# Linear attention followed by a gated feed-forward: even column blocks, cast loads, one-source preps and q prepared a block early

## The chip, the cores and the metric

The kernel runs on one core of a Trainium2 chip. The metric is device time in microseconds (us) from start to end of one execution; lower is better. TensorE (PE in the profile) multiplies, VectorE (DVE), ScalarE (ACT) and GpSimd (POOL) work element by element, SyncE (SP) issues DMAs. PE reads its operands from SBUF and writes to PSUM; DVE and ACT empty PSUM.

## The reference, cut to what matters

```python
# q, k, v: [8 batches, 8 heads, 576 rows, 64]; all float32
def phi(x, c, s):                    # c = cos, s = sin of the row's position
    r = np.maximum(x, 0.0)
    return np.concatenate([r * c, r * s], axis=-1)
q_p, k_p = phi(q, cos_w, sin_w), phi(k, cos_w, sin_w)
kv  = np.einsum('bhsf,bhsd->bhfd', k_p, v)
num = np.einsum('bhsf,bhfd->bhsd', q_p, kv)
den = np.einsum('bhsf,bhf->bhs', q_p, np.sum(k_p, axis=2))[..., None] + 1e-06
x = (num / den) ...                  # -> [4608 tokens, 512]
g = x @ w_gate                       # 512 -> 1536
out = (gelu(g) * (x @ w_val)) @ w_out    # 1536 -> 512
```

The 8 batches of 576 rows give 4608 tokens, and the feed-forward works on 9 blocks of 512 of them. Batch and block borders do not coincide, which is what half of the change is about.

## The kernel before

Words used below: a **prep** is relu times cos or sin (q or k to `qp`, `kp`). **Turning** q means transposing `qp` to `qT`, by a transposing DMA or on PE. **kv** is the k-v product, a **numerator** (`nm`) one of the five 128-row tiles of a batch, which DVE divides into `x_sb`, PE transposes and ACT copies to `xT`. A **gate unit** (`gv`) is one 128-wide slice of the hidden layer: 8 matmuls, gelu on ACT, product on DVE into `hT`. An **output step** is a third of an output tile: 4 matmuls.

```python
def cast_w(i):                                   # weights come as fp32 and are cast
    nc.scalar.copy(wg_sb[:, :, sl], wstage["wgf", i][:, :, 0:n * 128])
    nc.gpsimd.tensor_copy(wv_sb[:, :, sl], wstage["wvf", i][:, :, 0:n * 128])

def prep(name, b, pair, part, n=1):              # two sources in SBUF: src and the table
    for m in range(pair, pair + n):
        nc.vector.scalar_tensor_tensor(
            dst[:, m, :, part * D:(part + 1) * D], src[:, m % 2]..., 0.0,
            tab[:, :, None].to_broadcast([128, R, D]), op0=ALU.max, op1=ALU.mult)

def turn_q(b, pair0, n):                         # two transposing DMAs on SP
    for i in range(2):
        nc.sync.dma_start_transpose(out=qT[b][i]..., in_=src[64 * i:64 * i + 64, ...])

def gv_unit(c0, n, jt):
    gv_ps = psf.tile([128, 2, BLK], FP32, name="gv_ps")   # two buffers
    ...                                          # 4 gate and 4 value matmuls
    nc.scalar.activation(gel[:, 0:n], g_ps[:, 0:n], AF.Gelu)
    ...
    nc.vector.tensor_mul(hT[hb][:, jt, c:c + m], gel[:, o:o + m], v_ps[:, o:o + m])

# ... batch 0: preps, kv, all five tiles, then:
for jt in range(JT):                             # 12 gate units of columns 0 to 575
    gv_unit(0, 288, jt)
    gv_unit(288, 288, jt)
    ...                                          # casts; from jt 8 on: preps of batch 1, turn_q(1)
kv_unit(1)
attend_burst(1)                                  # batch 1 with nothing beside it
for i in range(4):
    o_part(i, range(JT), True)
segs = [(576, 448)] + [(BLK * i, BLK) for i in range(2, 9)]
for si, (c0, n) in enumerate(segs, start=1):
    b = si + 1                                   # the batch attended inside this block
    for jt in range(JT):
        gv_unit(c0, n, jt)
        s = jt - off                             # off: 3 in the first of them, else 0
        if s == 0: prep_pairs("qp", b, 0)
        if s == 1: prep_pairs("qp", b, 2)
        if s == 2: turn_q(b, 0, 4); prep_pairs("kp", b, 0)
        if s == 3: prep_pairs("kp", b, 2); cast_v(...)
        if s == 5: load_batch(b + 1); kv_unit(b)
        if 6 <= s < 11: nm_unit(b, s - 6)        # needs qT of this batch
        if 7 <= s < 12: xt_unit(b, s - 7)
        ...                                      # one output step of the block before
```

## Time and profile before

The time is 393.99 us (median of 2 runs, 392.53 to 395.44). The profiled execution spans 392.7 us. First come three lines of its page: busy times, and two lines of the span in 40 slices, where a digit is tenths of busy time (PE) or of full clock (PEclk).

```profile
PE 342.5 (87%) x2484; PEld 177.1 (45%) x2484; DVE 204.6 (52%) x379; ACT 128.7 (33%) x242; POOL 36.8 (9%) x35
PE   2588955899576988998999999979997999999995
PEclk9999986599888998999999999989999999999999
```

PE is the bound, but it is not busy throughout, and its granted clock is lower in the stretches with idle time (0.86 with 23 us idle, 1.00 with none, in the table). The next lines are a table of stretches: start and end, length, then busy time and count of PE, weight loads, DVE, ACT, POOL, the granted clock, DMA share and GB/s. The limits are the first gate matmul, the first gate of block 2 (column 1024), the first gate of block 7, and the start of the last four output tiles.

```profile
0.00:26.36 26.36, 13.06 (x168) 9.96 (x169) 18.10 (x30) 14.46 (x28) 11.67 (x15) 1.00 0.95 322
26.36:125.82 99.46, 76.41 (x604) 45.30 (x603) 52.85 (x110) 30.61 (x59) 15.45 (x12) 0.86 0.63 185
125.82:315.80 189.98, 180.48 (x1382) 89.14 (x1380) 116.87 (x215) 61.68 (x118) 9.66 (x9) 0.98 0.54 134
315.80:378.00 62.20, 62.20 (x290) 28.18 (x288) 16.32 (x25) 19.03 (x32) 0.00 (x0) 1.00 0.15 34
378.00:392.70 14.70, 10.34 (x48) 4.51 (x46) 0.47 (x1) 2.93 (x5) 0.00 (x0) 0.94 0.39 89
```

Blocks 7 and 8 (315.8 to 378.0) are the yardstick: no attention, PE busy all the time, 31.1 us a block. Blocks 2 to 6 each hold one batch's attention as well and take 189.98 / 5 = 38.0 us. The second row is the worst: clock 0.86 and 23 us without any matmul. What PE waited for in blocks 2 to 6 (engine and line, releaser, us in total, times, longest):

```profile
PE nm L260 <- DMA qT_1449<-qp: 2.6, 1, 2.6
PE nm L260 <- DMA qT_2744<-qp: 2.6, 1, 2.6
PE nm L260 <- DMA qT_3175<-qp: 2.5, 1, 2.5
PE nm L260 <- DMA qT_1881<-qp: 1.0, 1, 1.0
PE xt L309 <- DVE x_sb L273: 1.0, 1, 1.0
PE nm L260 <- DMA qT_2312<-qp: 0.8, 1, 0.8
```

Each block waits once, for its own batch's `qT`. The chain of waits shows why in block 2 (start, length, what):

```profile
137.38 1.73 PE gv_ps L332 x8
139.10 0.54 PE o_ps L370 x3
139.64 8.76 DMA qT_1449<-qp
148.39 0.04 issue
148.44 0.49 PE nm L260 x7
148.93 1.71 PE o_ps L370 x4
```

The second transposing DMA starts 13.8 us into the block and ends at 148.4, after the numerators were due.

### The profile page before, as it was taken

How to read it: one execution, taken by the hardware profiler on the slowest of the kernel's cores; microseconds unless marked ns; L12 is line 12 of the kernel's file. 1: busy time of each engine (PE TensorE's matmuls, PEld its weight loads, DVE VectorE, ACT ScalarE, POOL GpSimd, SP SyncE). 2: the span in 40 equal slices, each digit the busy share in tenths (PEclk: the TensorE clock that was granted, in tenths of full speed). 3: DMA queues.
4: the chain of work that ended last, by engine and by line, in shares of the span. 5: the costliest groups of instructions: out<-in, count | busy, mean ns of one | idle time of the engine just before them, and what ended most of it. 6: DMA issues, size and time to landing. Idle time of an engine off the chain costs nothing.

```text
span 392.7 us, 6081 instructions
## 1 busy us (share of the span) xinstructions
PE 342.5 (87%) x2484; PEld 177.1 (45%) x2484; DVE 204.6 (52%) x379; ACT 128.7 (33%) x242; POOL 36.8 (9%) x35
## 2 busy tenths in 40 slices
PE   2588955899576988998999999979997999999995
PEld 2365633544243444544544454535443544444442
DVE  6653496504945873587449556915693522222210
ACT  5755421213123331433333242314232333223321
POOL 1821530000202000200020011002000000000000
PEclk9999986599888998999999999989999999999999
DMA  8989908029495099309933990597056111111214
GB/s 265 381 278 362 388 15 120 2 66 357 65 222 214 2 142 321 128 1 126 340 126 44 192 350 6 86 246 258 2 84 118 29 27 42 40 27 28 52 42 95
DMA packets 57467, 55.83 MB, mean 142 GB/s; under 512 B 34912, under 2 KB 39008, under 8 KB 57440
## 3 DMA queue, kind: packets, MB, share of 16 engines
q1 hardware_dynamic: 57440, 55.45, 51.7%
q8 instruction: 19, 0.31, 0.3%
q14 instruction: 8, 0.07, 0.0%
HBM read 37.75 MB, written 9.44 MB: 120 GB/s over the span
## 4 chain that ended last, share of the span: by engine, by line
PE 71%; DMA 14%; DVE 8%; ACT 3%; POOL 2%; issue 1%; ACTq 0%; DVEq 0%; POOLq 0%
PE gv_ps L332 41%; PE o_ps L370 17%; PE gv_ps L370 6%; DVE qp L151 4%; PE xt L309 3%; PE nm L260 3%; DMA qT_1449<-qp 2%; DMA qT_3175<-qp 2%; DMA qT_2744<-qp 2%; DMA qT_1113<-qp 2%; DMA qT_702<-qp 2%; DMA qT_1881<-qp 2%; DVE hT L345 2%; DMA qT_2312<-qp 2%; DVE x_sb L273 1%; POOL pos L178 1%
## 5 line engine op out<-in xcount | busy, mean ns | idle before, releaser
L345 DVE TENSOR_TENSOR hT<-gel,gv_ps 128x512 bf16<-128x512 f32 (+2 forms) x132 | 76.0, 589 | 152.2 <-ACT gel L340 152.0
L340 ACT ACTIVATE gel<-gv_ps 128x512 f32<-128x512 f32 (+2 forms) x120 | 66.5, 555 | 203.9 <-PE gv_ps L332 203.0
L332 PE MATMUL gv_ps<-xT,wg_sb 128*128 128x512 bf16 x336 | 88.7, 388 | 0.0
L332 PE MATMUL gv_ps<-xT,wv_sb 128*128 128x512 bf16 x336 | 87.5, 383 | 0.0
L370 PE MATMUL o_ps<-wo_sb,hT 128*128 128x512 bf16 x336 | 87.1, 382 | 0.0
L332 PEld LDWEIGHTS <-wg_sb 128*128 128x128 bf16 x480 | 47.6, 101 | 64.0 <-issue 18.0
L332 PEld LDWEIGHTS <-wv_sb 128*128 128x128 bf16 x480 | 48.6, 101 | 49.9 <-issue 4.2
L370 PEld LDWEIGHTS <-hT 128*128 128x128 bf16 x432 | 41.2, 100 | 44.7 <-issue 3.5
L332 PE MATMUL gv_ps<-xT_335,wg_sb 128*128 128x288 bf16 (+1 forms) x144 | 30.0, 335 | 11.2 <-DVE hT L345 10.9
L332 PE MATMUL gv_ps<-xT_335,wv_sb 128*128 128x288 bf16 (+1 forms) x144 | 30.3, 339 | 0.0
L151 DVE SCALAR_TENSOR_TENSOR qp<-qf,cos_t 128x576 bf16<-128x576 f32 x32 | 26.0, 849 | 2.5 <-DMA qf<-in_q_dram 2.4
L151 DVE SCALAR_TENSOR_TENSOR kp<-kf,cos_t 128x576 bf16<-128x576 f32 x32 | 25.9, 851 | 1.5 <-DMA kf<-in_k_dram 1.5
L273 DVE TENSOR_TENSOR x_sb<-nm,rec 128x512 bf16<-128x512 f32 x34 | 23.5, 692 | 1.2
L370 PE MATMUL gv_ps<-wo_sb,hT 128*128 128x512 bf16 x96 | 23.3, 407 | 0.0
L151 DVE SCALAR_TENSOR_TENSOR kp<-kf,sin_t 128x576 bf16<-128x576 f32 x30 | 22.3, 788 | 0.0
L151 DVE SCALAR_TENSOR_TENSOR qp<-qf,sin_t 128x576 bf16<-128x576 f32 x30 | 21.4, 752 | 0.0
L309 PE MATMUL xt<-ident,x_sb 128*128 128x128 bf16 x144 | 15.6, 238 | 4.2 <-DVE x_sb L273 3.2
L187 POOL CAST vx_132<-vf 128x1152 bf16<-128x1152 f32 x7 | 8.7, 1250 | 112.1 <-DMA vf<-in_v_dram 77.9
L379 ACT COPY o_sb<-o_ps 128x512 f32<-128x512 f32 x28 | 16.4, 586 | 7.4 <-PE o_ps L370 7.4
L187 POOL CAST vx_134<-vf 128x1152 bf16<-128x1152 f32 x8 | 9.2, 1150 | 102.0 <-DMA vf<-in_v_dram 102.0
L317 ACT COPY xT<-xt 128x512 bf16<-128x512 bf16 (+1 forms) x34 | 16.7, 501 | 4.8 <-PE xt L309 4.7
L237 PEld LDWEIGHTS <-kp 64*128 64x128 bf16 x576 | 11.0, 100 | 9.7 <-issue 4.0
(77 smaller groups left out, 171.9 us busy)
## 6 DMA issues: line engine op xcount, KB each, us to landing
out_dram<-o_sb SPq DMA_DIRECT2D x72, 128.0 KB, 2.4
qf<-in_q_dram SPq DMA_DIRECT2D x14, 576.0 KB, 5.0
kf<-in_k_dram SPq DMA_DIRECT2D x14, 576.0 KB, 7.2
vf<-in_v_dram SPq DMA_DIRECT2D x14, 576.0 KB, 9.7
wgf<-in_moe_w_gate_dram SPq DMA_DIRECT2D x4, 768.0 KB, 6.6
wvf<-in_moe_w_val_dram SPq DMA_DIRECT2D x4, 768.0 KB, 7.8
wof<-in_moe_w_out_dram SPq DMA_DIRECT2D x4, 768.0 KB, 12.6
qf<-in_q_dram SPq DMA_DIRECT2D x4, 288.0 KB, 4.1
```

Source lines behind the costliest of these rows:

```text
L151: nc.vector.scalar_tensor_tensor(dst[:, m, :, part * D:(part + 1) * D], src[:, m % 2].rearrange("p (j d) -> p j d", j=R), 0.0, tab[:, :, N ...
L187: copy(vx_tiles[b % 2][:, 2 * half:2 * half + 2, :, 0:D], staged["vf", b, half].rearrange("p m (j d) -> p m j d", j=R),)
L237: nc.tensor.matmul(ps[:, i, pair * (D + 1):(pair + 1) * (D + 1)], lhsT=kp[rr, pair, j, :], rhs=vx[rr, pair, j, :], start=(j == 0), stop=(j ...
L260: nc.tensor.matmul(ps[:, h // 4, (h % 4) * (D + 1):(h % 4 + 1) * (D + 1)], lhsT=qT[b][h % 2][:, h // 2, c0:c0 + 128], rhs=kv_sb[b][:, h // ...
L273: nc.vector.tensor_tensor(x, nm[:, :, :, 0:D], rec[:, :, :, None].to_broadcast([128, 2, 4, D]), op=ALU.mult,)
L309: nc.tensor.transpose(out=ps[:, ct, :], in_=x[:, ct * 128:(ct + 1) * 128], identity=ident)
L317: nc.scalar.copy(xt[:, :, base + c:base + c + m], ps[:, :, o:o + m])
L332: nc.tensor.matmul(ps[:, 0:n], lhsT=w[:, ct, js], rhs=xt[:, ct, cc:cc + n], start=(ct == 0), stop=(ct == CT - 1),)
L340: nc.scalar.activation(gel[:, 0:n], g_ps[:, 0:n], AF.Gelu)
L345: nc.vector.tensor_mul(hT[hb][:, jt, c:c + m], gel[:, o:o + m], v_ps[:, o:o + m])
L370: nc.tensor.matmul(o_ps[i], lhsT=hT[blk][:, jt, tt * 128:(tt + 1) * 128], rhs=wo_sb[:, jt, :], start=(jt == 0), stop=(jt == JT - 1),)
L379: nc.scalar.copy(o_sb, o_ps.pop(i))
```

## The change

Its intent: give every block the same 512 columns (the first eight units of block 0 as two runs of 256, so that gates can start with two tiles); load weights by a casting DMA on GpSimd's queue, held back by a tiny copy (`probe`) until k has landed; make the preps one-source operations (all but the first ones of batch 0); turn q of batches 1 and 2 on PE; thread the attention of batches 0 to 2 into gate units; and prep and turn q of batch b+1 at the end of the block that attends batch b, its load being issued a further block ahead. The core of the diff:

```diff
-    wst = ctx.enter_context(tc.tile_pool(name="wst", bufs=4))
-    inp = ctx.enter_context(tc.tile_pool(name="inp", bufs=3))
+    inp = ctx.enter_context(tc.tile_pool(name="inp", bufs=1))
@@ weights
+    def load_w(jt0, n):
         sl = slice(jt0 * 128, (jt0 + n) * 128)
-        nc.scalar.copy(wg_sb[:, :, sl], wstage["wgf", i][:, :, 0:n * 128])
-        nc.gpsimd.tensor_copy(wv_sb[:, :, sl], wstage["wvf", i][:, :, 0:n * 128])
+        nc.gpsimd.dma_start(out=wg_sb[:, :, sl], in_=wg_r[:, :, sl])
+        nc.gpsimd.dma_start(out=wv_sb[:, :, sl], in_=wv_r[:, :, sl])
@@ preps
+        for j in range(j0, j1):
+            for part, tab in enumerate((cos_t, sin_t)):
+                nc.vector.tensor_scalar(
+                    dst[:, m:m + n, j, part * D:(part + 1) * D],
+                    src[:, m:m + n, j],
+                    0.0,
+                    tab[:, j:j + 1],
+                    op0=ALU.max,
+                    op1=ALU.mult,
+                )
@@ order (cut)
+    probe = consts.tile([128, 1], FP32)
+    nc.gpsimd.tensor_copy(probe, staged["kf", 0][:, 2, 0:1])
+    load_w(0, 2)
     ...
+    for jt in range(8):
+        gv_unit(0, 256, jt)
     ...                                  # tiles 2 to 4 of batch 0 in between
+    for jt in range(8):
+        gv_unit(256, 256, jt)
+        if jt >= 5:
+            prep("qp", 1, 3 * (jt - 5), 3 * (jt - 4))
+    for jt in range(8, JT):
+        gv_unit(0, BLK, jt)
+        if jt < 11:
+            turn_q_pe(1, 3 * (jt - 8), 3)
     ...
+    for jt in range(JT):
+        gv_unit(BLK, S - BLK, jt)        # 64 columns; batch 1 attended in between
     ...
+    for jt in range(JT):
+        gv_unit(S, 2 * BLK - S, jt)      # 448 columns; batch 2 and output tiles 0 to 3 in between
     ...
+    for i in range(3):
+        prep_step("qp", 3, i)
+    turn_q(3, 0, NP)
+    for blk in range(2, 9):
+        b = blk + 1
         for jt in range(JT):
+            gv_unit(BLK * blk, BLK, jt)
     ...                                  # kp preps in units 0 to 2, kv in 5, numerators from 6
+                if b + 1 < B and jt >= 9:
+                    prep_step("qp", b + 1, jt - 9)
+                    if jt == 11:
+                        turn_q(b + 1, 0, NP)
```

## The prediction

> **What bounds it now.** TensorE work that cannot shrink. In the chain of waits a steady 512-column step is 1.73 us of gate/value and 0.86 us of output matmuls, 216 ns each. 864 + 432 of them are 280 us; attention of batches 1 to 7 adds about 4.5 us each (kv 2.0 us, five numerator-and-transpose pairs at 0.5 us: steps of 3.07 instead of 2.59). So 311 us are needed after the first gate matmul, which starts at 26.4 us, and 4.4 us of tail. The span is 392.7: 50 us are lost. By the table of stretches:
> - 26.4 to 125.8 us (columns 0 to 1023, output tiles 0 to 3, attention 1 and 2): 99.5 us for 61 us of matmul work. Waits: gates for DVE products queued behind 0.75 us preps (10.9 us), the transposing DMAs of q (7.2 us chain pieces at 61.9 and 106.7), and a 26.6 us stretch at granted clock 0.72 where attention of batch 1 runs alone.
> - 125.8 to 315.8 (blocks 2 to 6): 38.0 us a block; TensorE idles 9.5 us, mostly for q transposes, and one group after such a wait runs 3.41 instead of 1.73 us.
> - After 315.8: dense, nothing to win.
>
> **What the change does.**
> 1. Blocks 2 to 6: q is prepped and turned one block earlier. The transposing DMA (6 to 8.8 us to landing) gets about 15 us. Gain: 9.5 us idle plus 2.5 of clock.
> 2. Head: weights skip fp32 staging (12 casts of 1.47 us on ACT and POOL go), two of five tiles of batch 0 precede the first gate; kp stays on DVE (8 x 0.67 us). First gate at about 20: gain 6.
> 3. Columns 0 to 1023: attention of batches 0 to 2 is threaded through gate units, q of batches 1 and 2 turned on TensorE. Work from 20 us: 41.5 gates, 10.4 outputs, 10.5 attention, 5.3 for 92 transposes, 2.6 because 64-column gates run at the 54 ns spacing of the 65-column numerators: 70 us. I allow 14 us of stalls (single-buffered chains at the end of block 1, about 2 us a tile; the 64-column loop bound by DVE, 1.3 us a step; weight waits). Ends at 104 instead of 125.8.
> 4. Preps become one-source operations of 256 elements, 18 per tensor. The Trainium skill, "VectorE: DVE Perf Modes", Mode 2x_2P: one source and destination in SBUF allow two elements a cycle, fp32 too. Then about 0.2 us each (estimate; 576 elements now take 0.67), a tensor 3.7 instead of 5.4 us. DVE is 52% busy; this only smooths.
> 5. Weights by cast DMA, 9.4 MB in one GpSimd queue with q1, k1, v1. The skill's "DMA: Bandwidth & Descriptors", Measured, gives 341 GB/s for 1 MB from GpSimd; plain loads ran at 322 GB/s here. No trace here shows a cast DMA. At 300 GB/s units 0 to 7 are in by 24 us, the rest by 36: just in time.
>
> **Sum.** 104 + 178 (five blocks of 35.6) + 62.2 + 10.4 + 4.4 = 359 us.
>
> **Prediction:** 359 us, 348 to 373 in 8 of 10. Faster by over 2%: 0.95; within 2%: 0.04; slower: 0.01.
>
> **Signs.** No wait for qT in blocks 2 to 6, each about 35.6 us; block 2 starts at about 104; first gate at about 20; clock near 1.0 after the first run; preps near 0.2 us.
>
> **What would make it wrong.** Cast DMA at half rate: units 5 to 11 wait for W, 10 to 15 us more. GpSimd's descriptors held up by DVE's two-port preps. Clock drops in the 64-column loop. Fewer stalls would give 350.

## The result, and the profile after

The changed kernel takes 360.54 us (median of 2 runs, 359.94 to 361.14), against 393.99 before. The ratio is 0.915 (95% interval 0.899 to 0.931). A ratio is the mean time of one kernel's fast runs over the mean time of the other kernel's fast runs of the same rounds, so it is not quite the ratio of the medians.

The same kernel was run once more, unaltered, beside the experiments. What had been expected of that run:

> The changed kernel itself, unaltered, so that its time stands beside the variants on the same chip in the same rounds. Expected: 360 to 361 us, ratio 0.915 to 0.920 to the kernel before.

It took 360.24 us (median of 4), ratio 0.917 (0.912 to 0.921).

The same three lines of the page, for the changed kernel:

```profile
PE 325.2 (91%) x2582; PEld 174.5 (49%) x2620; DVE 193.1 (54%) x529; ACT 132.0 (37%) x247; POOL 30.2 (8%) x51
PE   2477895799989999999999999999999999999994
PEclk9999998999999999999999999999999999999999
```

The table of stretches, at the same five events:

```profile
0.00:20.72 20.72, 7.03 (x113) 5.22 (x114) 10.85 (x25) 9.32 (x14) 9.53 (x22) 1.00 0.98 234
20.72:105.95 85.23, 73.22 (x787) 48.36 (x792) 53.92 (x167) 39.25 (x83) 10.11 (x14) 0.98 0.65 186
105.95:280.70 174.75, 172.74 (x1359) 88.23 (x1382) 111.57 (x314) 61.53 (x114) 10.52 (x17) 1.00 0.58 141
280.70:342.88 62.18, 61.87 (x284) 28.15 (x288) 16.30 (x25) 19.01 (x32) 0.00 (x0) 1.00 0.15 34
342.88:358.20 15.32, 10.30 (x47) 4.50 (x46) 0.49 (x1) 2.93 (x5) 0.00 (x0) 1.00 0.39 86
```

| stretch | before, us | predicted | after, us | saved |
|---|---|---|---|---|
| to the first gate | 26.4 | 20 | 20.7 | 5.6 |
| first gate to block 2 | 99.5 | 84 | 85.2 | 14.2 |
| blocks 2 to 6 | 190.0 | 178 | 174.8 | 15.2 |
| the rest | 76.9 | 77 | 77.5 | -0.6 |
| span | 392.7 | 359 | 358.2 | 34.5 |

All that PE waited for in blocks 2 to 6 is now this:

```profile
PE o_ps L331 <- issue: 0.8, 5, 0.2
PE gv_ps L298 <- DVE hT L309: 0.2, 1, 0.2
```

The waits for `qT` are gone and the clock stays at 1.00. In the second stretch, PE idles 12 us instead of 23 and the clock is 0.98 instead of 0.86. That is where the change still loses time; the experiments look into both stretches.

### The profile page after: what moved, and what is told of

Its sections match the earlier page's. It is cut to its first block, busy times and chain, and to the rows that moved or that the text cites. A ratio compares the mean times of both kernels' runs of the same rounds, so it can differ in the third digit from the quotient of the medians.

```text
span 358.2 us, 6436 instructions
## 1 busy us (share of the span) xinstructions
PE 325.2 (91%) x2582; PEld 174.5 (49%) x2620; DVE 193.1 (54%) x529; ACT 132.0 (37%) x247; POOL 30.2 (8%) x51
## 4 chain that ended last, share of the span: by engine, by line
PE 82%; DVE 9%; ACT 3%; DMA 2%; issue 2%; SPq 1%; ACTq 0%
PE gv_ps L298 48%; PE o_ps L331 21%; PE nm L214 3%; PE gv_ps L331 3%; PE nm L233 3%; DVE qp L131 3%; DMA vf<-in_v_dram 2%; DVE x_sb L246 2%; PE xt L277 2%; DVE hT L309 2%; PE nm L178 1%; ACT gel L306 1%; DVE kp L131 1%; DVE rec L245 1%; SPq L68 1%
## 5 line engine op out<-in xcount | busy, mean ns | idle before, releaser
L309 DVE TENSOR_TENSOR hT<-gel,gv_ps 128x512 bf16<-128x512 f32 (+3 forms) x128 | 77.1, 603 | 137.4 <-ACT gel L306 137.2
L306 ACT ACTIVATE gel<-gv_ps 128x512 f32<-128x512 f32 (+3 forms) x128 | 67.9, 531 | 177.5 <-PE gv_ps L298 177.5
L298 PE MATMUL gv_ps<-xT,wg_sb 128*128 128x512 bf16 (+3 forms) x498 | 114.7, 348 | 6.5 <-DVE hT L309 4.9
L298 PE MATMUL gv_ps<-xT,wv_sb 128*128 128x512 bf16 (+3 forms) x501 | 113.2, 348 | 0.6
L331 PE MATMUL o_ps<-wo_sb,hT 128*128 128x512 bf16 x372 | 96.6, 379 | 1.1 <-issue 0.8
L131 DVE TENSOR_SCALAR qp<-qf,sin_t 128x256 bf16<-128x256 f32 x68 | 24.2, 356 | 0.0
L131 DVE TENSOR_SCALAR qp<-qf,cos_t 128x256 bf16<-128x256 f32 x68 | 24.0, 353 | 0.0
L131 DVE TENSOR_SCALAR kp<-kf,sin_t 128x256 bf16<-128x256 f32 x63 | 22.0, 349 | 0.0
L131 DVE TENSOR_SCALAR kp<-kf,cos_t 128x256 bf16<-128x256 f32 x63 | 22.0, 349 | 0.0
L277 PEld LDWEIGHTS <-x_sb 128*128 128x128 bf16 x160 | 10.2, 99 | 7.9 <-DVE x_sb L246 6.4
## 6 DMA issues: line engine op xcount, KB each, us to landing
vf<-in_v_dram POOLq DMA_DIRECT2D x2, 1152.0 KB, 15.1
```

The lines of the kernel that those rows point to most:

```text
L131: nc.vector.tensor_scalar(dst[:, m:m + n, j, part * D:(part + 1) * D], src[:, m:m + n, j], 0.0, tab[:, j:j + 1], op0=ALU.max, op1=ALU.mult,)
L277: nc.tensor.transpose(out=ps[:, ct, :], in_=x[:, ct * 128:(ct + 1) * 128], identity=ident)
L298: nc.tensor.matmul(ps[:, 0:n], lhsT=w[:, ct, js], rhs=xt[:, ct, cc:cc + n], start=(ct == 0), stop=(ct == CT - 1),)
L309: nc.vector.tensor_mul(hT[blk][:, jt, cc:cc + n], gel[:, 0:n], v_ps[:, 0:n])
L331: nc.tensor.matmul(o_ps[i], lhsT=hT[blk][:, jt, tt * 128:(tt + 1) * 128], rhs=wo_sb[:, jt, :], start=(jt == 0), stop=(jt == JT - 1),)
```

## The experiments

Differences to the changed kernel are given as the difference of the two ratios times 393 us, because the experiments ran on more than one chip. The 95% intervals of these ratios reach 0.004 to 0.008 to each side (1.4 to 3.1 us). The smallest differences rest on more than that: the rerun above and the variants of the q load, of the one run and of the turn by DMA ran on one chip in the same rounds, and no time of the three lies within those of the rerun. For the weights not held back and for the first rearranged variant the marks in the profiles point the same way. Positions in the schedule come from the profiles; the first kv matmul of a block is a good mark.

### Turning q in its own block again

```diff
-                if jt < 3:
-                    prep_step("kp", b, jt)
+                if b > 3:
+                    if jt == 0:
+                        prep("qp", b, 0, 6)
+                    if jt == 1:
+                        prep("qp", b, 6, R)
+                        turn_q(b, 0, NP)
+                    if 2 <= jt < 5:
+                        prep_step("kp", b, jt - 2)
 ...
-                if b + 1 < B and jt >= 9:
-                    prep_step("qp", b + 1, jt - 9)
-                    if jt == 11:
-                        turn_q(b + 1, 0, NP)
```

> The changed kernel (360.5 us), but q of batches 4 to 7 is prepped and turned in its own block again, as the kernel before did; the one-source preps stay. Theory (turning q a block early is what took the wait out of blocks 2 to 6): numerators of blocks 3 to 6 wait for qT again, 2 to 3 us each plus some clock, so 368 to 373 us, and these four blocks read about 37 to 38 us instead of 34.9. Rival (the faster one-source preps alone would have removed the wait): under 363 us, blocks under 35.6 us, no wait for qT over 0.5 us.

The edit also puts 12 of the 18 preps of q into unit 0. Measured: 365.78 us, ratio 0.932, that is 6.0 us more than the changed kernel. What PE waits for in blocks 2 to 6:

```profile
PE nm L233 <- DMA qT<-qp: 3.9, 3, 1.8
PE gv_ps L298 <- DVE hT L309: 0.3, 1, 0.3
```

The waits for `qT` are back, in three of the four altered blocks. The last output tiles start at 348.30 instead of 342.88 us, so an altered block takes 34.9 + 5.4 / 4 = 36.2 us. Both theories missed: 36.2 lies between the under 35.6 of the rival and the 37 to 38 of mine. In the four blocks the wait falls from 6.9 us (before) to 3.9. The first transposing DMA of a block is issued 6.1 us ahead of its kv here and 5.7 ahead in the kernel before, so the rest of the change, the faster preps among it, brings the turn forward a little and shortens the wait; it does not remove it.

### The early turn alone, in the kernel before

```diff
+                if si <= 2:
                     if s == 0: prep_pairs("qp", b, 0)
                     if s == 1: prep_pairs("qp", b, 2)
                     if s == 2: turn_q(b, 0, 4)
 ...
+                if si >= 2 and b + 1 < B:
+                    if s in (9, 10):
+                        prep_pairs("qp", b + 1, 2 * (s - 9))
+                    if s == 11:
+                        turn_q(b + 1, 0, 4)
```

> The kernel before (394 us), with one part of the change alone: q of batches 4 to 7 prepped and turned one block early (old preps, old loads). Theory: the qT waits of blocks 3 to 6 go, 382 to 386 us, these blocks at about 35 us instead of 38. Rival (needs the one-source preps or the earlier q load as well): 390 us or more.

Measured: 385.53 us, ratio 0.981 (0.974 to 0.988), 7.5 us less than before, clear of no gain but not of a gain under 2%: as my theory had it. Of the waits of PE in blocks 2 to 6 these are left; the one for `qT` is block 2's, which this edit leaves alone:

```profile
PE xt L309 <- DVE x_sb L273: 3.4, 4, 1.6
PE nm L260 <- DMA qT<-qp: 1.7, 1, 1.7
```

From kv to kv the altered blocks take 35.65 us. So the early turn alone takes a block from 38.0 to 35.65, the rest of the change without it comes to 36.2, and both together to 34.9. The two overlap: they cure the same wait. The rest of the change holds the one-source preps, but also fewer and larger loads of q, k and v; one-source preps alone in the kernel before were not run. What the early turn alone leaves (3.4 us, once in each of four blocks) is PE waiting for `x_sb`, which on DVE stands behind the long preps of the next q.

### Two-source preps

```diff
-        for j in range(j0, j1):
+        for mm in range(m, m + n):
             for part, tab in enumerate((cos_t, sin_t)):
-                nc.vector.tensor_scalar(
-                    dst[:, m:m + n, j, part * D:(part + 1) * D],
-                    src[:, m:m + n, j],
+                nc.vector.scalar_tensor_tensor(
+                    dst[:, mm, j0:j1, part * D:(part + 1) * D],
+                    src[:, mm, j0:j1],
                     0.0,
-                    tab[:, j:j + 1],
+                    tab[:, j0:j1, None].to_broadcast([128, j1 - j0, D]),
```

> The changed kernel, but all preps of its loops are two-source operations again (8 of 192 elements a step instead of 6 of 256). DVE is 22 of 34.9 us busy in a steady block, so theory: blocks 2 to 6 stay at 34.9 us within 0.2; only the stretch 42 to 112 us, where DVE stands on the chain of waits, gets longer: 362 to 366 us in all. Rival (the preps were the main gain): 370 us or more, with steady blocks at 36 us or more.

Measured: 367.47 us, ratio 0.935, 7.1 us more. From kv to kv the steady blocks take 35.12 us (34.86 in the changed kernel), so they hardly care, as expected (0.26 us, a little over the 0.2 allowed). The first kv of a steady block comes at 125.85 instead of 121.05 us: 4.8 of the 5.8 us between the two profiles are lost before block 2, where DVE is on the chain of waits. The total is above my range and below the rival's; the size was under-estimated, the place was right. "DVE is 52% busy; this only smooths", as the prediction put it, was wrong for the stretch from the first gate to block 2.

### q loaded with its k and v

```diff
     def load_batch(b):
+        if b > 3:
+            load(nc.sync, "qf", q, b)
         load(nc.sync, "kf", k, b)
         load(nc.sync, "vf", v, b)
-        if b + 1 < B:
-            load(nc.sync, "qf", q, b + 1)
```

> The changed kernel, but q of batches 4 to 7 is loaded together with its k and v, at unit 5 of the block in which it is prepped at unit 9. Theory (what counts is when q is turned, not when it is loaded; a load lands in 5 to 11 us and the prep comes about 11 us after its issue): as the changed kernel, within 1.5 us. Rival (the two-batch distance of the load is needed): the preps wait for q, 2 us or more a block, 368 us or more.

Measured: 361.21 us, ratio 0.919, 0.8 us more, inside the 1.5 us allowed; kv to kv stays at 34.86 us. Issuing the load a further block ahead is a part of the change that bought less than 1 us; turning early is what counts.

### Block 0 as one run

```diff
     nm_unit(0, 0)
     nm_unit(0, 1, True)
     xt_unit(0, 0)
     xt_unit(0, 1, True)
+    ...                                  # preps, turns and tiles 2 to 4 of batch 0
     for jt in range(8):
-        gv_unit(0, 256, jt)
-    ...
-    for jt in range(8):
-        gv_unit(256, 256, jt)
+        gv_unit(0, BLK, jt)
         if jt >= 5:
             prep("qp", 1, 3 * (jt - 5), 3 * (jt - 4))
```

> The changed kernel, but all five tiles of batch 0 are attended before the first gate and block 0 is one run of 512 columns. Theory: first gate 6 us later (about 27 us), but the 256-column units, which run at 0.98 instead of 0.87 us because of two PSUM buffers, and the threaded small steps go: 362 to 366 us in all. Rival (the two runs hide the weight load, so one run must stall on W or lose all six): 366 us or more.

Measured: 362.43 us, ratio 0.922, 2.0 us more: within my range. Its first gate comes at 30.42 us, 9.7 us later than in the changed kernel (I had expected 6), yet its first 64-column unit starts at 54.53 us, against 53.37 in the changed kernel. So almost all of the early start is given back by the first run itself. There the small steps of tiles 2 to 4 stand in PE's order between short units, and several wait 0.3 to 0.8 us for DVE or ACT. From the first gate to the first 64-column unit PE is busy 28.9 of 32.7 us in the changed kernel, and 24.0 of 24.1 us in this variant, where tiles 2 to 4 are done before. Starting 9.7 us earlier was worth 2 us.

### Weights not held back

```diff
-    nc.gpsimd.tensor_copy(probe, staged["kf", 0][:, 2, 0:1])
+    nc.gpsimd.memset(probe, 0.0)
```

> The changed kernel, but the small GpSimd copy that holds the weight loads back until the second half of k has landed is replaced by a memset, so the weights are issued at once. Theory (the copy is what lets q, k and v of batch 0 land first): v lands 3 to 5 us later, the first gate comes 2 to 4 us later, 362 to 365 us; this would also explain most of the 3.6 us by which the first gate of the staged variant was late. Rival (order does not matter, the loads share the rate anyway): within 1 us of the changed kernel.

Measured: 364.01 us, ratio 0.925, 3.4 us more, as expected. The chains to the first gate begin with a load of v of batch 0; here is that piece in the changed kernel, then in this one:

```profile
3.16 8.82 DMA vf<-in_v_dram
12.00 1.17 ACT vx_124 L155
```

```profile
4.24 13.63 DMA vf<-in_v_dram
17.90 0.67 ACT vx L155
```

v is loaded and cast in pieces, and the two chains do not run through the same piece. The last piece lands at 17.87 instead of 13.45 us, 4.4 us later. The first gate comes at 24.67 instead of 20.72 us, and all later marks keep that distance (first steady kv at 125.39 instead of 121.05). A delay of the first gate that shifts the whole chain is paid in full, unlike the one of the experiment before, which moved work from after the gate to before it.

### Weights through fp32 staging

```diff
-        nc.gpsimd.dma_start(out=wg_sb[:, :, sl], in_=wg_r[:, :, sl])
-        nc.gpsimd.dma_start(out=wv_sb[:, :, sl], in_=wv_r[:, :, sl])
+            t = wst.tile([128, CT, 384], FP32, name=name, tag="w")
+            nc.sync.dma_start(out=t, in_=src[:, :, sl])
 ...
+        nc.scalar.copy(wg_sb[:, :, sl], wstage["wgf", i])
+        nc.gpsimd.tensor_copy(wv_sb[:, :, sl], wstage["wvf", i])
```

> The changed kernel, but weights go through fp32 staging on the SP queue and casts on ACT and POOL again. Theory (cast DMA is a convenience worth little): the casts stand before or between the first gates, 362 to 367 us, everything after 60 us as before. Rival (the cast DMA carries the head and the first stretch): 372 us or more.

Measured: 367.12 us, ratio 0.934, 7.0 us more, at the edge of my range. This variant has no `probe`, and its first gate is late by 3.6 us, nearly as in the experiment before. Against that one it is 3.1 us slower (367.12 - 364.01, the same chip), and that is about what cast DMA is worth; the casts then stand on ACT and POOL among the first gates. The variant also loads the weights in other pieces, and q1, k1 and v1 on SP, so the 3.1 us are not of the cast alone.

### q of batches 1 and 2 turned by DMA

```diff
-        if jt < 11:
-            turn_q_pe(1, 3 * (jt - 8), 3)
+        if jt == 8:
+            turn_q(1, 0, NP)
 ...
-        if jt in (4, 5, 6):
-            turn_q_pe(2, 3 * (jt - 4), 3)
+        if jt == 4:
+            turn_q(2, 0, NP)
```

> The changed kernel, but q of batches 1 and 2 is turned by the transposing DMA instead of on TensorE. Theory (the DMA was harmful before only because nothing ran ahead of it; here 10 us or more lie between): no wait for qT, 72 transposes of 56 ns and 12 copies go, 356 to 360 us. Rival (turning on TensorE is what saved this stretch): waits for qT of 2 us or more twice, 364 us or more.

Measured: 358.21 us, ratio 0.911 (0.908 to 0.915), 2.1 us less than the changed kernel. The turn on PE, part of the change, costs time: there is room for the DMA once q is prepped early. No wait of PE for `qT` is left in its profile.

### Batch 3's q inside block 1

On top of the variant before:

```diff
         if jt == 4:
             turn_q(2, 0, NP)
+            load(nc.sync, "qf", q, 3)
+        if jt >= 9:
+            prep_step("qp", 3, jt - 9)
 ...
-    for i in range(3):
-        prep_step("qp", 3, i)
     turn_q(3, 0, NP)
```

> The DMA-turned variant (358.2 us), and q of batch 3 is loaded during block 1 and prepped in its units 9 to 11 instead of in one run of 18 operations (5.2 us) between blocks 1 and 2. Theory (these 18 operations hold up the first products of block 2 by about 5 us): 353 to 356 us, block 2 without the wait of gates for DVE products. Rival (two PSUM buffers already cover it, or the preps only move the hold-up into block 1): 357 us or more.

Measured: 363.39 us, ratio 0.924: 4.8 us more than the variant that it builds on. The expectation failed. The edit issues q3's load on SP behind two transposing DMAs, so a late q3 that holds up DVE is the likely cause, but that is argued, not shown. The profile fell on a slow run (579.89 us at a mean granted clock of 0.573; the others took 362.59 to 364.20), and in it PE is so slow that nothing comes late. The DMA times of that profile support the argument, though: q3 lands 15.1 us after the last prep of q2 (98.1 to 113.2 us), and the only `qp` buffer is free 10.8 us after it. In the fast profile of the variant before, that prep ends at 80.9 us and the preps of q3 would be due from 90.9, behind the product of unit 9. By this estimate q3 comes at about 96.0, some 5 us late. That the preps only moved the hold-up into block 1, the rival, is not excluded. The next variants load q3 well ahead and have the same preps in units 9 to 11.

### The stretch rearranged

The 64-column units go. After block 0, the output steps of block 0 are run with batch 1's attention in between, then block 1 as 512 columns with batch 2's attention. q of batches 1 to 3 is turned by DMA; ACT does the sin half of the k preps of batches 1 and 2.

```diff
-    for jt in range(JT):
-        gv_unit(BLK, S - BLK, jt)
-    ...
-        gv_unit(S, 2 * BLK - S, jt)
+    for i in range(JT):
+        o_step(0, i)
+        if i == 1:
+            kv_unit(1)
+        if i in (0, 1, 2):
+            prep_step("qp", 2, i)
+        if i == 2:
+            turn_q(2, 0, NP)
+        if 3 <= i < 8:
+            nm_unit(1, i - 3)
+        if 4 <= i < 9:
+            xt_unit(1, i - 4)
+    ...
+    for jt in range(JT):
+        gv_unit(BLK, BLK, jt)
+        ...                              # kv(2) in unit 3, numerators from 4, qp of 3 from 9
```

> The changed kernel with the stretch from 36 to 112 us rearranged: no 64-column units; block 1 is one run of 512 columns; batch 1 is attended between the output matmuls of block 0; q of batches 1 to 3 is turned by DMA and prepped ahead; half of the preps of k of batches 1 and 2 on ACT. Counting matmul work from 36 us as 54 us and 5 us of stalls, block 2 should start at 95 to 99 instead of 106 us: 348 to 354 us. If the chain of DVE products only moves, 356 us or more.

Measured: 357.15 us, ratio 0.907, 3.7 us less than the changed kernel, but short of the range. The first steady kv comes at 119.53 us, only 1.5 us earlier. The chain of waits names the reason:

```profile
45.33 7.81 PE gv_ps L298 x32
53.14 8.30 DMA qT<-qp
61.57 4.82 DVE qp L131 x18
66.73 0.70 DVE x_sb L246
```

The preps of q2 wait for the DMA that still reads q1 out of the only `qp` buffer, and the numerators of batch 1 stand behind those preps on DVE. DVE's own list of waits has this one from 40 to 80 us:

```profile
DVE qp L131 <- DMA qT<-qp: 4.7, 1, 4.7
```

### The same without its own stall

```diff
-            phi[name, b] = attn.tile([128, NP, R, F], BF16, name=name)
+            phi[name, b] = attn.tile(
+                [128, NP, R, F], BF16, name=name, bufs=2 if name == "qp" else 1
+            )
 ...                                     # q1 prepped in units 1 to 5; numerators from step 4
     for jt in range(JT):
+        if 6 <= jt < 6 + NT:
+            xt_unit(2, jt - 6)
+        if 5 <= jt < 5 + NT:
+            nm_unit(2, jt - 5)
         gv_unit(BLK, BLK, jt)
-        if 4 <= jt < 4 + NT:
-            nm_unit(2, jt - 4)
-        if 5 <= jt < 5 + NT:
-            xt_unit(2, jt - 5)
```

> The rearranged variant (357.2 us) with its own stall taken out. In its chain of waits the preps of q2 wait 4.7 us for the transposing DMA of q1 to finish reading the one qp buffer, and the numerators of batch 1 queue on DVE behind those preps (4.7 us more). Here qp has two buffers, q1 is prepped two units earlier, the numerators start one step later, and in block 1 a tile's numerator comes before the gate unit, so that its product does not stand behind that unit's activation. Theory: 9 us of that stretch and 2 us of block 1 go, 345 to 351 us. Rival (DVE has no room there, the wait only moves): 354 us or more.

Measured: 350.93 us (349.35 to 351.33), ratio to the kernel before 0.889 (0.884 to 0.895). Its result is correct, and it beats both kernels: 10.8 us below the changed one. The first steady kv comes at 112.19 instead of 121.05 us. DVE's wait for the transposing DMA is gone, and the stretch from the first gate to block 2 takes 75.8 us (85.2 in the changed kernel). The edit makes four small moves at once; what each is worth was not run.

| run | us | ratio to before | against the changed kernel, us |
|---|---|---|---|
| changed kernel again | 360.24 | 0.917 | 0 |
| q turned in its own block | 365.78 | 0.932 | +6.0 |
| two-source preps | 367.47 | 0.935 | +7.1 |
| staged weights | 367.12 | 0.934 | +7.0 |
| early turn alone, in before | 385.53 | 0.981 | |
| q loaded with k and v | 361.21 | 0.919 | +0.8 |
| block 0 as one run | 362.43 | 0.922 | +2.0 |
| turned by DMA | 358.21 | 0.911 | -2.1 |
| weights not held back | 364.01 | 0.925 | +3.4 |
| q3 inside block 1 | 363.39 | 0.924 | +2.7 |
| rearranged | 357.15 | 0.907 | -3.7 |
| rearranged, stall removed | 350.93 | 0.889 | -10.8 |

## Why the prediction was right or wrong, point by point

The prediction, 359 us, was met: 360.5 us in the timed runs and 358.2 in the profile. Counting the matmul work that remains and pricing each stretch by it worked. Not every step of the sum was right, though; some errors cancel.

1. **Blocks 2 to 6: right in kind, mis-sized.** I expected 35.6 us a block and 12 us of gain; measured were 34.95 (174.75 / 5) and 15.2 us. The term that was off is kv. I took its 72 matmuls at 2.0 us from the head of the kernel, where the trace has 2.16 us; in the steady blocks they take 1.33 us, in both kernels. Here they are in the kernel before, at its head and in block 2:

```profile
16.79 2.16 PE L237 MATMUL nm<-vx_132,kp 64*128 64x65 bf16 x72 [3.99 <-POOL vx_132 L187]
141.79 1.33 PE L237 MATMUL nm<-vx_134,kp 64*128 64x65 bf16 x72
```

   Five times 0.7 us is 3.5 us, which covers the gap (178 - 174.75 = 3.25). In the prediction's other words, idle time and clock: PE's idle time fell by 7.5 us and its busy time by 7.7 (180.48 to 172.74), where 9.5 and 2.5 were expected. So matmuls that run slowly around a wait, like the four of 1.71 us above, cost more than was read from them. The cause was also credited to the early turn alone. The runs show that the rest of the change shortens the same wait (38.0 to about 36.2 us a block without the early turn, 35.65 with the early turn alone).

2. **Head: the place was right, the credit was not.** The first gate came at 20.7 us, as predicted at about 20. But the prediction booked the 6 us as a gain. The one-run experiment starts the gates 9.7 us later and loses 2.0 us. What did pay in the head is the hold on the weight loads (3.4 us), which the prediction does not mention.

3. **From the first gate to block 2: right, by two errors.** Predicted 70 us of work and 14 of stalls, 84 in all; measured 85.2. The work was over-counted. The 54 ns are those of numerators at the slow head of the kernel before (53 ns at 19.7 us); from block 2 on, most of its numerators take 32 ns. Of the 96 gate and value matmuls of 64 columns, 72 take about 29 ns (four in 0.12 us) and the others about 50, so some 1.9 of the 2.6 us extra are not there, and kv of two batches is 1.4 us less at the steady rate. That leaves about 67 us of work (70 - 1.9 - 1.4, an estimate), hence about 18 us of stalls and slow matmuls, 12.0 of them idle time of PE. The rearranged variants show that much of this was not necessary. The two over-counts have one root, as in point 1: a cost was read where PE ran slowly and used for where it does not. That the total came out right is in part luck.

4. **Preps: wrong about their worth.** "This only smooths" failed before block 2: 4.8 of the 5.8 us between the profiles of that experiment are lost there. The 52% are a mean over the whole span and say nothing of a stretch in which DVE is on the chain. The estimate of 0.2 us for one was low too: the trace has 0.26 us from start to start.

5. **Cast DMA: right.** No gate waited for weights. The whole of the gate and value weights and q1, 7.47 MB read (6.29 + 1.18), came between 11.1 and 34.6 us, 318 GB/s; units 0 to 7 were in by 26.7 us (24 predicted), the rest by 34.6 (36). The casts avoided were worth about 3 us.

6. **What would make it wrong.** The clock held (0.90 in the 64-column stretch, 1.00 later). GpSimd's DMA issues took 0.75 to 0.89 us throughout, so DVE did not hold them up noticeably; the reverse happened, shown below.

The parts do not add up exactly to the 34.5 us, since they overlap (the early turn and the rest of the change in blocks 2 to 6 most of all). What the threading of the attention into the gate units is worth by itself was not run alone and stays open.

## What to carry to other kernels

When the bound engine's work cannot shrink, price each stretch of the trace by that work; what is left over is the stall that a change can remove, and two cures for one stall must not be added. A slow transfer is harmless when what feeds it runs a whole block ahead: move the producer and the turn, not only the load. An earlier start of the main work is worth little (2.0 of 9.7 us here) if the work moved behind it comes back as small dependent steps in the main engine's order. And read the cost of a step where the engine runs at full pace, not at the head of the kernel.

## What the Trainium skill lacked or had wrong

- "DMA: Bandwidth & Descriptors", section Measured, lists loads from GpSimd (341 GB/s at 1 MB) and does not say that any of them casts. Here casting loads with one plain load among them read 318 GB/s, an estimate from 7.47 MB in 23.5 us, while the end of v of batch 0 and the start of k of batch 1 were moved as well.
- The same page, section Latency and other measured facts, gives 261 GB/s for a transposing DMA with a strided middle dimension. Here one such DMA turned 590 KB (64 partitions x 4608 two-byte elements) in 6.0 us from issue to landing at best (in the variant with staged weights), an estimate of 98 GB/s; a pair in the kernel before took 10.5 us from the first issue to the second landing, an estimate of 112 GB/s. A plan that took the page's figure would start the turn too late.
- "TensorE: Matmul & The Clock Gate", section Back-to-back issue gap, gives about 131 ns as the sustained spacing at 512 columns. In every dense block here it is 216 ns (8 in 1.73 us), which is what the formula for the isolated gap in the same section says. At 64 columns most matmuls follow each other by about 29 ns although every one has a new weight load, close to the 25 ns floor of its table.
- The same page, Part 1, says that a cold array runs at half rate for about 3.4 us and warns that the clock events of a trace can be unreliable. This agrees and is no lack: the first gates of the changed kernel take 0.85 us for four 256-column matmuls up to 24.1 us, 3.4 us after the first, and 0.44 from 25.3 us on, while the granted clock of the profile reads 1.00 from 20.72 to 26 us.
- "VectorE: DVE Perf Modes", section Side-by-side, has the same fixed cost in all modes. Here a two-source prep of 256 elements takes 0.334 us from start to start (one of 576 takes 0.668, so 1.04 ns an element) and a one-source prep of 256 takes 0.262 us. If the latter runs at two elements a cycle, the parts that do not grow with the elements are about 0.07 and 0.13 us (estimates), so the double rate saves 0.07 us and not 0.13. One-source preps of another size were not run, so a lower rate with the same fixed cost is not excluded.
- "SBUF — State Buffer", in its box on DVE and DMA, describes DVE's two-port operations holding up the descriptors that GpSimd writes. The general rule in its section Who interferes with whom, that the first to issue keeps the shared port, also covers the reverse, and the trace of the changed kernel fits it: of three preps that start during a DMA issue on POOL, two end 0.1 us after that issue, having taken 0.68 and 0.58 us instead of 0.34 (the third starts 0.11 us into the issue and takes 0.34). Beside casts on POOL it is the same: in the last variant eight preps between 41.7 and 72.2 us take 0.63 to 0.83 us.

```profile
23.13 0.83 POOL L84 DMA_DIRECT2D wo_sb<-in_moe_w_out_dram  x1 [1.81 <-DMA wv_sb<-in_moe_w_val_dram]
23.37 0.68 DVE L131 TENSOR_SCALAR qp<-qf,cos_t 128x256 bf16<-128x256 f32 x1
24.98 0.85 POOL L84 DMA_DIRECT2D wo_sb<-in_moe_w_out_dram  x1 [1.02 <-DMA wg_sb<-in_moe_w_gate_dram]
25.35 0.58 DVE L131 TENSOR_SCALAR qp<-qf,sin_t 128x256 bf16<-128x256 f32 x1
```

- No page consulted here speaks of a single-core run whose granted clock stays near half although PE is busy. One of the four runs of a variant did: it took 579.89 us instead of 363, at 0.73 in the first 60 us, at 0.55 to 0.56 from then on, and at 0.573 on average.
